# One fused attention and Fourier-mixing kernel: the planner's constants, one new rule for GpSimd, and the instruction order that follows from them

## The chip, the core and the metric

The kernel runs on one core of one Trainium2 chip. The metric is the device time of one execution in microseconds; 672.24 us is the median of three runs of the kernel before (668.16 to 672.58).

## What is computed

The first half is a delta-rule recurrence for 4 batches of 8 heads (768 steps, head size 48), the second half mixes its output by Fourier transforms and sends it through a two-layer MLP. All of it is float32.

```python
for t in range(S):                       # deltanet, per batch and head
    y[t] = q[t] @ state
    v_old = state.T @ k_n[t]             # k_n: k over its norm
    state = state + beta[t] * outer(k_n[t], v[t] - v_old)
# bridge: heads side by side -> x (4, 768, 384)
mixed = real(fft(fft(x, axis=1), axis=2))
u = x + mixed
un = (u - mean(u)) / sqrt(var(u) + 1e-6)
out = u + maximum(un @ w_ch1, 0) @ w_ch2   # 384 -> 1536 -> 384
```

## The kernel before

**Tiles.** The recurrence is done in chunks. A unit is 128 steps of one batch with all 8 heads, two chunks of 64; there are 24 units, six per batch, and six buffers `us` for them. Units go through in rounds: round 0 has units 0 to 3, round 1 units 4 and 5 (together batch 0), rounds 2 to 7 three units each.

**Stages of a round.** K and Q are turned on TensorE (`turn`, transposes, L480), the products of keys and queries are made (`gram`, `keys`, results cleared by L696, L707 and copies at L486), and a triangular system is inverted on VectorE by a long chain of small instructions: `begin16`/`invert16` for rounds 0 and 1 (transposes L795, pairs L855 and L861, transposes L881 and L878), `begin`/`invert` for the others (L751, L766, pairs L933 and L938, L950). `blocks`, `ahead`, `step` and `outputs` then use the inverse unit by unit (L960, L966, L1190, L1219, L1254).

**Batch 0.** It has its own chain, `chain0`: eleven updates of the state, one after another. Each is a small matmul of the state (`st,R`), a copy of two halves of `u` out of PSUM, a matmul of keys and `u`, and a copy of the new state `st` (both copies at L486 on ScalarE, or L488 on VectorE). After the last output (`x`, L486) come the mixing of batch 0 (folds L1279, matmuls with `tab` and `ft`, statistics L1393, scaling L1409, transposes of `pm`) and its MLP, groups of twelve matmuls `R,w` (first layer) and eight `w,R` (second layer) as the hardware counts them: a float32 matmul of the program is two on the chip, a transpose one. The same follows for batches 1 to 3, and matmuls of the MLP are laid between the small matmuls of the next batch's recurrence.

**The weights.** `w_ch1` and `w_ch2` come as 64-bit numbers in 18 pieces of 512 columns. A piece is loaded into a staging place on the SP queue, then converted: L1795 and L1801 on ScalarE, L1798 and L1806 on VectorE, an addition on GpSimd (L1811), and L1814 on VectorE. GpSimd does little else. `where` (L1986) gives the staging place: the first `NW` = 8 pieces use a ring of seven places in `ws`, `x1`, `R1` and `R0`, the others a ring of three. From the eighth piece on a transfer is cut in rows 0 to 120 and 121 to 127 (L1786).

**The order.** No engine's order is written by hand. Every operation is given to `Plan` with a duration for each engine that may run it, its reads and writes, its PSUM banks and a due time; `schedule` walks through planned time and gives each free engine the ready operation with the least `pr`, and `issue` emits all in that order. Each engine then runs its list in order, whatever the real times are. Some rules are built in:

- a VectorE operation marked `port` (a conversion of weights, some folds) is not started while GpSimd's addition runs, and the other way round;
- PE may wait for a better operation that is nearly ready (`PLOOK`, `PHOLD`);
- where PE has nothing ready for `GAP` (inside the listed spans) or `GAP2`, or its activity over the last `SPANW` microseconds falls below `TARGET` (`FORCE` before 20 us), a filler is issued (L2036, L2043): a matmul whose result nobody reads, to keep up TensorE's clock. Before `HALF` the filler may be a pair of 64 rows;
- `speed` doubles planned PE time in windows of 3.413 us after one with too little activity.

Due times come from `due_a` and `due_m` with the constants `M0` to `MD`; `pick` chooses between small and large matmuls with `WAIT`, `GATHER`, `URGENT`.

Of the kernel before, what the change touches and what calls it, by code (L numbers as in the profile page):

```python
# [29 lines left out]
SHARE = 0.3  # L30
RATE = 190.0
WIN, WARM, COLD, BUSY, CLOCK = 3.413, 610.0, 619.0, 200.0, True
LOOK, HOLD, EARLY = 1e9, 0.2, 25.7
FOLD, BY, SEQ, HOT, HOTPE, HOTPK, HOTG, NORM = 1, 1, 2, 1.0, 1, 1, 0, 1
HOTC, PORT, E2 = 2, 1, 5.0
GAP, HALF = 0.198, 68.4
LATE = 0.0
GAP2 = 0.304
PLOOK, PHOLD, PEND = 23.4, 0.367, 116.9
NHALF = 1  # L40
FORCE = 540.9
BLOCK, LEAD, SEEK, LAND, HOLDUP = 256, 60, 1.0, 2.4, 0.0
CUT, ROW = 512, 121
PLAIN, W1T = {(2, 2): (0, 1, 2, 3, 4, 5), (3, 2): (4, 5)}, 0.112
WF = 2, 2
TARGET, SPANW = 692.9, 2.6


class Plan:
# [102 lines left out]
    def light(self, now):  # L152

        a = now - SPANW
        self.past = [p for p in self.past if p[1] > a]
        return sum(c * (min(e, now) - max(s, a)) for s, e, c in self.past) < (TARGET if now > 20 else FORCE) * SPANW

    def schedule(self, pick, limits, switch, idle=None, span=()):
# [15 lines left out]
        free = {e: 0.0 for e in self.ENG}  # L174
# [8 lines left out]
                    avail[e].append(o)  # L183
        self.win, self.sum, self.cold, self.past, self.hist = 0.0, 0.0, True, [], []
        self.count, self.come = 64, [0.0, 0.0]
        self.bursts = []
        done, n, now = 0, len(ops), 0.0
        order, strict, last = [], True, None
        while done < n:
            progressed = False  # L190
            for e in self.ENG:
# [52 lines left out]
                elif cand:  # L244
# [10 lines left out]
                    if best and strict and LOOK and e in ("DVE", "ACT"):  # L255

                        x = now + best.engs[e] - HOLD
                        y, z = best.pr - (LOOK if now > EARLY else 1.0), best.pr - HOT
# [5 lines left out]
                    continue  # L264
                o = best
                dur = o.engs[e]
                if e == "PE":
                    dur *= self.speed(now)
                    if mode is not None:
                        dur += switch.get((mode, o.mode), 0.0)  # L270
                    mode = o.mode
                    for b, s in zip(o.new, fr[len(o.new), o.mode] if o.new else ()):
                        b.slot, slots[s] = s, None
                        self.half = {k: x for k, x in self.half.items() if x != s}
                        held[b.cls] = held.get(b.cls, 0) + 1
# [39 lines left out]
            if not progressed:  # L315
# [7 lines left out]
                now, strict = min(nxt, default=now), bool(nxt)  # L323
# [55 lines left out]
def kernel(  # L379
# [36 lines left out]
    P = Plan(nc, tc, 8)  # L416
# [39 lines left out]
    def A(t, c0, c1, p0=0, p1=128):  # L456
        t, o = parts.get(id(t), (t, 0))
        c0, c1 = c0 + o, c1 + o
        return (id(t), p0, p1, c0, c1)
# [10 lines left out]
    def eng(e):  # L470
        return {"DVE": nc.vector, "POOL": nc.gpsimd, "ACT": nc.scalar, "SP": nc.sync}[e]

    def I(x):
        kp(x)
# [17 lines left out]
    def t_dve(n, ps=False):  # L492
        return 0.07 + n * 1.04e-3

    def t_act(n):
        return 0.07 + n * 0.84e-3

    def t_pool(n):
        return 0.20 + n * 1.9e-3
# [23 lines left out]
    def dma(o, i, wr, pr, rd=(), kb=200, q="SP"):  # L523
        def fn(e):
            I((nc.sync if q == "SP" else nc.scalar).dma_start(out=o, in_=i))
        P.op({q: 0.45}, fn, rd, wr, pr, lat=2.0, kb=kb)


    M0, MP, MX, MN, MA, MT, MD = 91.8, 128.0, 19.9, 38, 17.7, 5.85, 4.52

    def due_a(b, T):
        if b == 0:
# [65 lines left out]
    def pads(ap, acc, pr):  # L598
        def fn(e):
            I(eng(e).memset(ap, 0.0))  # L600
        P.op({"POOL": 0.3, "DVE": 0.2}, fn, [], [acc], pr, lat=LP)
# [1159 lines left out]
    nw = [0]  # L1761

    def weights(src, dst, rows, cols, where, pr, pieces=None):


        n = 512
        if src.dtype == F32:
            d = dst.rearrange("p (c f) -> p c f", c=rows)
            for r in sorted({c0 // cols for c0 in pieces}):
                dma(d[:, r], src[128 * r:128 * r + 128, :], [A(dst, cols * r, cols * r + cols)], pr)  # L1770
            return
        sv = src.bitcast(I32).rearrange("(c p) (f two) -> p (c f) two" if False else
                                        "(c p) f2 -> p c f2", p=128)
        for c0 in pieces:
            w0 = where(nw)
            nw[0] += 1
            st = w0[0][:, w0[1]:w0[1] + 2 * n]
            a0 = A(w0[0], w0[1], w0[1] + 2 * n)
            cc = dst[:, c0:c0 + n]
            ac = A(dst, c0, c0 + n)  # L1780
            rr = st[:, 0:2 * n:2]
            done = 0
            while done < n:
                r, c = divmod(c0 + done, cols)
                m = min(n - done, cols - c, CUT)
                for x0, x1 in ((0, ROW), (ROW, 128)) if nw[0] > 7 else ((0, 128),):  # L1786
                    dma(st[x0:x1, 2 * done:2 * done + 2 * m].bitcast(I32),
                        sv[x0:x1, r, 2 * c:2 * c + 2 * m],
                        [A(w0[0], w0[1] + 2 * done, w0[1] + 2 * done + 2 * m, x0, x1)], pr,
                        kb=m * (x1 - x0) / 128)  # L1790
                done += m
            lo, hi = st[:, 0:2 * n:2], st[:, 1:2 * n:2]

            def f0(e, cc=cc, hi=hi):
                I(nc.scalar.activation(cc, hi, ACT.Abs))  # L1795

            def f1(e, cc=cc):
                I(eng(e).tensor_scalar(cc, cc, LB, UB, op0=ALU.max, op1=ALU.min))  # L1798

            def f2(e, rr=rr, lo=lo):  # L1800
                I(nc.scalar.activation(rr.bitcast(I32), lo.bitcast(U32), ACT.Copy,  # L1801
                                       scale=2.0 ** -29))

            def f3(e, cc=cc):
                w = cc.bitcast(I32)
                I(nc.vector.tensor_scalar(w, w, 5, 2, op0=ALU.logical_shift_left,  # L1806
                                          op1=ALU.logical_shift_right))

            def f4(e, cc=cc, rr=rr):
                w = cc.bitcast(I32)  # L1810
                I(nc.gpsimd.tensor_tensor(w, w, rr.bitcast(I32), op=ALU.add))  # L1811

            def f6(e, cc=cc, hi=hi, c0=c0):
                I(nc.vector.scalar_tensor_tensor(  # L1814
                    dst[:, c0:c0 + n].bitcast(I32), hi.bitcast(I32), -2 ** 30, cc.bitcast(I32),
                    op0=ALU.bitwise_and, op1=ALU.bitwise_xor))
            P.op({"ACT": t_act(n) + 0.07}, f0, [a0], [ac], pr, lat=LA)
            P.op({"DVE": 0.38}, f1, [], [ac], pr, lat=LD, port=True)
            P.op({"ACT": t_act(n) + 0.07}, f2, [], [a0], pr, lat=LA)
            P.op({"DVE": 0.40}, f3, [], [ac], pr, lat=LD, port=True)  # L1820
            P.op({"POOL": t_pool(n) + 0.2}, f4, [a0], [ac], pr, lat=LP, port=True)
            P.op({"DVE": t_dve(n) + 0.03}, f6, [a0], [ac], pr, lat=LD, port=True)
# [3 lines left out]


    nb = [0]
    NW, IV, IV1, WP = 8, 18.9, 9.07, -14.4

    dma(pack, cn["pack"].ap(), [PK], -300, q="ACT", kb=130)
    dma(bt, beta.rearrange("b h s -> (b h) s"), [aBT], -250, q="ACT", kb=98)
# [3 lines left out]
    pads(half, A(half, 0, 1), 0)  # L1836
    for w in p_:
        pads(w, A(w, 0, 256), -400)

    def eps(e):  # L1840
        I(eng(e).memset(half, 1e-6))
# [27 lines left out]
    def mixing(b):  # L1869
        pr = 0  # L1870
        P.hot = True
        for t in range(TH):
            folds(b, t, pr)
        tag = [(("last", b), 0, 1, 0, 1)]
        for i in range(2):
            seq(b, i, pr, tag)
        for T in range(NT):
            feat(b, T, pr)
        for g in range(NT // 2):
            for T in (2 * g, 2 * g + 1):  # L1880
                normed(b, T, pr)
            P.hot = False
            if (b, g) >= WF:
                if b == B - 1:
                    mlpw(b, g, pr)
            else:
                mlp(b, g, pr)
            P.hot = g < HOTG
        P.hot = False
# [35 lines left out]
    def consume(ro):  # L1925
        for i, z in enumerate(ro.us):
            pr = 0
            blocks(z, i, ro, pr)
            ahead(z, pr)
            step(z, 0, pr)  # L1930
            step(z, 1, pr)
            outputs(z, pr)
            if z.T == NT - 1 and z.b:
                if z.b == B - 1:
                    sums1(0)
                    for g in range(NT // 2):
                        if (B - 2, g) >= WF:
                            mlpw(B - 2, g, 0)
                mixing(z.b)
# [46 lines left out]
    def where(nw):  # L1986
        return stages[nw[0] % 7] if nw[0] < NW else stages[(nw[0] - NW) % 3]
# [9 lines left out]
        consume(ro)  # L1997

    LIM = {"state": 1, "sum": 4, "attn": 6, "mix": 4, "mlp": 4, "norm": 2, "win": 4}
    WAIT, GATHER, URGENT, FIRST = 6.3, 1.59, 8.45, 15  # L2000
    E0, E1, D1 = 1.0, 10.0, 125.6
    seen = {}

    def pick(cand, mode, now, free):
# [24 lines left out]
    def idle(two, mode, now):  # L2029
# [3 lines left out]
        def fn(e):  # L2033
# [12 lines left out]

    SW = {("128", "64"): 0.1, ("64", "128"): 0.21, ("128", "T"): 0.1, ("T", "128"): 0.05,
          ("64", "T"): 0.15, ("T", "64"): 0.1}
    P.schedule(pick, LIM, SW, idle, ((E0, D1),))
    P.issue()  # L2050


# [28 lines left out]
```

## Time and profile before

| what | value |
|---|---|
| runs | 672.58, 668.16, 672.24 us |
| the profiled execution's own time | 667.22 us |
| its span, first to last instruction | 665.4 us |
| PE busy, VectorE busy, ScalarE busy, GpSimd busy | 650.6, 504.1, 270.3, 36.3 us |
| granted TensorE clock, mean | 0.997 |
| instructions | 23378 |

A busy PE is not PE at its peak: matmuls are pipelined and their ends are modelled. So times between the starts of matmuls are used as well. Times in the views are counted from the span's start. The engines are PE (matmuls) with PEld (weight loads), DVE (VectorE), ACT (ScalarE), POOL (GpSimd) and SP, whose queue issues the transfers. "x" is a number of instructions.

### The profile page before, as it was taken

To read this page: it belongs to the slowest core of one execution; us is meant where nothing else is said; L and a number is where in the kernel's file an instruction comes from. 1 tells how busy PE (TensorE), PEld (TensorE's weight loads), DVE (VectorE), ACT (ScalarE), POOL (GpSimd) and SP (SyncE) were. 2 spreads that over 40 slices of the span, in tenths; PEclk is the share of its full clock that TensorE was granted. 3 is DMA by queue.
4 is the path that set the end of the run, shared out by engine and by line. 5 is a ranking of instruction groups with operands and counts; after the bars stand their busy time and mean duration, and the time that the engine had idled before them with its cause. 6 is when DMAs were issued, how large, how long until landed. Compare 5 with 4: busy or idle time off the path is not lost.

```text
span 665.4 us, 23378 instructions
## 1 busy us (share of the span) xinstructions
PE 650.6 (98%) x10184; PEld 535.8 (81%) x10184; DVE 504.1 (76%) x1479; ACT 270.3 (41%) x758; POOL 36.3 (5%) x34
## 2 busy tenths in 40 slices
PE   8998899999899999999999999999999999999998
PEld 7888888777678777877777778777777789999997
DVE  3998589999964399999922589998981865877473
ACT  5579787621354332524333433244324313321220
POOL 3004223130000000000000000000000000000000
PEclk9999899999999999999999999999999999999999
DMA  9905565100033113001212120000000000000000
GB/s 201 304 33 105 146 142 148 35 0 25 1 63 75 38 26 73 1 1 26 63 38 50 50 49 2 24 2 3 26 2 3 26 3 0 25 1 25 1 25 25
DMA packets 82667, 31.38 MB, mean 47 GB/s; under 512 B 75651, under 2 KB 79716, under 8 KB 82436
## 3 DMA queue, kind: packets, MB, share of 16 engines
q1 hardware_dynamic: 82372, 29.65, 18.0%
q8 instruction: 80, 1.31, 0.8%
q10 hardware_dynamic: 192, 0.23, 0.1%
q14 instruction: 23, 0.19, 0.1%
HBM read 25.16 MB, written 4.72 MB: 45 GB/s over the span
## 4 chain that ended last, share of the span: by engine, by line
PE 80%; DVE 13%; ACT 3%; issue 2%; DMA 1%; DVEq 0%; SPq 0%; ACTq 0%
PE pp L477 75%; PE pp L480 3%; DVE rr L938 2%; DVE tmp L933 2%; ACT us L486 1%; PE pp L2043 1%; PE pp L2036 1%; DMA x<-in_moe_w_ch_dram 1%; DVE rr L795 1%; DMA us<-in_q_dram 1%; DVE tmp L855 1%; DVE w L861 1%; DVE us L714 0%; ACT w L1795 0%; DVE us L696 0%
## 5 line engine op out<-in xcount | busy, mean ns | idle before, releaser
L477 PE MATMUL pp<-R,w 128*128 128x256 f32 (+1 forms) x832 | 184.1, 368 | 0.6 <-ACT R L486 0.6
L477 PEld LDWEIGHTS pp<-R,w 128*128 128x128 f32 x832 | 145.1, 190 | 19.7 <-ACT R L486 0.7
L477 PE MATMUL pp<-w,R 128*128 128x384 f32 x384 | 135.1, 495 | 0.0
L477 PEld LDWEIGHTS pp<-w,R 128*128 128x128 f32 x384 | 70.0, 190 | 41.0 <-issue 0.2
L486 ACT ACTIVATE us<-pp 128x256 f32<-128x256 f32 (+3 forms) x186 | 65.0, 388 | 61.6 <-PE pp L477 48.3
L1475 ACT ACTIVATE R<-pp 128x512 f32<-128x512 f32 x48 | 28.7, 597 | 106.8 <-PE pp L477 106.8
L477 PE MATMUL pp<-us 64*64 64x48 f32 (+3 forms) x2496 | 61.7, 235 | 1.6 <-issue 1.3
L938 DVE TENSOR_TENSOR rr<-rr,tmp 128x108 f32<-128x108 f32 (+13 forms) x180 | 57.6, 330 | 2.3
L477 PEld LDWEIGHTS pp<-us 64*64 64x64 f32 (+1 forms) x2496 | 52.3, 136 | 8.7 <-issue 5.5
L933 DVE TENSOR_TENSOR tmp<-rr 128x210 f32<-128x210 f32 (+12 forms) x180 | 57.3, 328 | 2.1
L1190 DVE TENSOR_TENSOR u<-u,pp 64x192 f32<-64x192 f32 x66 | 22.4, 351 | 39.3 <-PE pp L477 37.7
L477 PEld LDWEIGHTS pp<-u,us 64*64 64x64 f32 x1472 | 39.7, 134 | 14.7 <-issue 10.5
L477 PE MATMUL pp<-u,us 64*64 64x48 f32 x1472 | 45.7, 221 | 2.8 <-issue 1.3
L486 ACT ACTIVATE x<-pp 64x192 f32<-64x192 f32 (+1 forms) x81 | 25.2, 324 | 54.2 <-PE pp L477 50.1
L1254 DVE TENSOR_TENSOR x<-x,pp 64x192 f32<-64x192 f32 x66 | 23.2, 351 | 24.5 <-PE pp L477 23.3
L486 ACT ACTIVATE R<-pp 128x192 f32<-128x192 f32 (+7 forms) x80 | 22.5, 333 | 43.0 <-PE pp L477 21.8
L1650 DVE TENSOR_TENSOR us<-us,pp 128x256 f32<-128x256 f32 x64 | 26.7, 418 | 12.5 <-ACT us L486 10.3
L477 PE MATMUL pp<-tab,R 128*96 128x193 f32 (+2 forms) x192 | 33.0, 328 | 0.1
L477 PEld LDWEIGHTS pp<-st,us 48*64 48x64 f32 x1232 | 22.6, 134 | 12.3 <-issue 9.8
L477 PEld LDWEIGHTS pp<-tab,R 128*96 128x96 f32 (+2 forms) x192 | 30.8, 163 | 1.4 <-DVE R L1279 0.6
L2043 PE MATMUL pp<-pack 64*64 64x256 f32 (+1 forms) x206 | 31.1, 384 | 0.0
L486 ACT ACTIVATE u<-pp 64x192 f32<-64x192 f32 (+1 forms) x68 | 22.2, 326 | 17.0 <-PE pp L477 11.7
(165 smaller groups left out, 978.1 us busy)
## 6 DMA issues: line engine op xcount, KB each, us to landing
out_dram<-x SPq DMA_DIRECT2D x11, 384.0 KB
us<-in_k_dram SPq DMA_DIRECT2D x16, 192.0 KB
us<-in_q_dram SPq DMA_DIRECT2D x16, 192.0 KB
us<-in_v_dram SPq DMA_DIRECT2D x16, 192.0 KB
us<-in_v_dram SPq DMA_DIRECT2D x8, 181.5 KB
ws<-in_moe_w_ch_dram SPq DMA_DIRECT2D x3, 484.0 KB
us<-in_k_dram SPq DMA_DIRECT2D x8, 181.5 KB
us<-in_q_dram SPq DMA_DIRECT2D x8, 181.5 KB
```

What stands on the lines that cost most here:

```text
L477: I(nc.tensor.matmul(o, lhsT=lhsT, rhs=rhs, start=start, stop=stop, skip_group_check=True))
L480: I(nc.tensor.matmul(o, lhsT=src, rhs=ident[p0:p0 + n, p0:p0 + n], is_transpose=True, start=start, stop=True, skip_group_check=True))
L486: I(nc.scalar.activation(o, i, ACT.Copy, **({} if scale is None else {"scale": scale})))
L795: vec(1760, lambda e: I(nc.vector.transpose(R, ro.gd(0, 4).rearrange("p (n c) -> p c n", c=32))), [ro.agd(0, 4)], [aR], pr)
L855: I(eng(e).tensor_tensor(T_, sub(j + 1, 16, j, j + 1).broadcast_to([128, 2, n, j]), sub(j, j + 1, 0, j).broadcast_to([128, 2, n, j]), op=A ...
L933: I(eng(e).tensor_tensor(T_, R[:, :, j + 1:32, j:j + 1].broadcast_to([128, ns, n, j]), R[:, :, j:j + 1, 0:j].broadcast_to([128, ns, n, j]) ...
L938: I(eng(e).tensor_tensor(R[:, :, j + 1:32, 0:j], R[:, :, j + 1:32, 0:j], T_, op=ALU.add))
L1190: I(nc.vector.tensor_tensor(U[:, s], U[:, s], psum(b1[s])[a, s0:s1].rearrange("p (j d) -> p j d", d=D), op=ALU.subtract))
L1254: I(nc.vector.tensor_tensor(w, w, v, op=ALU.add))
L1475: I(nc.scalar.activation(o, s, ACT.Relu))
L1650: vec(256, lambda e: I(nc.vector.tensor_tensor(o, i0(), i1(), op=ALU.add)), [], [aH] + list(wr), pr - EV, use=n)
L2043: I(nc.tensor.matmul(pst[two[0]][x, 0:256], lhsT=w[x, 0:n], rhs=w[x, 0:256], start=True, stop=True, skip_group_check=True))
```

## The change

About twenty constants of the planner get other values. A new rule adds 0.9 us (`CHARGE`) to the planned duration of the first VectorE operation without a PSUM bank that starts while GpSimd's addition runs. A second span, 250 to 280 us of planned time, is treated as the first one is: there PE's activity is watched and fillers are issued after shorter gaps. In `consume`, `blocks` and `ahead` of the second and third unit of a round are made more urgent by 4.3 us each. The ring of seven staging places now serves the first 15 pieces of the weights; the row cut begins after the seventh piece or the `NW`-th, whichever is less.

```diff
-LOOK, HOLD, EARLY = 1e9, 0.2, 25.7
+LOOK, HOLD, EARLY = 1e9, 0.204, 22.8
...
-GAP, HALF = 0.198, 68.4
+GAP, HALF = 0.198, 71.5
...
-PLOOK, PHOLD, PEND = 23.4, 0.367, 116.9
+PLOOK, PHOLD, PEND = 58.7, 0.317, 115.6
...
-FORCE = 540.9
+FORCE = 579.1
 BLOCK, LEAD, SEEK, LAND, HOLDUP = 256, 60, 1.0, 2.4, 0.0
+CHARGE = 0.9
...
-TARGET, SPANW = 692.9, 2.6
+TARGET, SPANW = 690.0, 2.6
...
-        self.bursts = []
+        self.bursts, self.lock = [], 1e9
...
+                if e == "POOL" and o.port:
+                    self.lock = now + 0.2
+                if e == "DVE" and not o.banks and self.lock < now < free["POOL"]:
+                    self.lock, dur = 1e9, dur + CHARGE
...
-    M0, MP, MX, MN, MA, MT, MD = 91.8, 128.0, 19.9, 38, 17.7, 5.85, 4.52
+    M0, MP, MX, MN, MA, MT, MD = 86.9, 139.9, 29, 37.9, 19.8, 5.91, 5.44
...
-                for x0, x1 in ((0, ROW), (ROW, 128)) if nw[0] > 7 else ((0, 128),):
+                for x0, x1 in ((0, ROW), (ROW, 128)) if nw[0] > min(7, NW) else ((0, 128),):
...
-    NW, IV, IV1, WP = 8, 18.9, 9.07, -14.4
+    NW, IV, IV1, WP = 15, 18.9, 6.6, -14.4
...
+    BL = 4.3
...
-            blocks(z, i, ro, pr)
-            ahead(z, pr)
+            blocks(z, i, ro, -BL * i)
+            ahead(z, -BL * i)
...
-    WAIT, GATHER, URGENT, FIRST = 6.3, 1.59, 8.45, 15
-    E0, E1, D1 = 1.0, 10.0, 125.6
+    WAIT, GATHER, URGENT, FIRST = 5.29, 2.53, 5.88, 15
+    F0, F1 = 250.0, 280.0
+    E0, E1, D1 = 1.0, 10.0, 129.8
...
-    P.schedule(pick, LIM, SW, idle, ((E0, D1),))
+    P.schedule(pick, LIM, SW, idle, ((E0, D1), (F0, F1)))
```

In what follows line numbers are those of the kernel before; in the kernel after the same lines stand 5 to 7 lines further down.

## The prediction

> **What bounds the kernel now.** First the page's table of slices, to see where an engine is full:
>
> ```profile
> PE   8998899999899999999999999999999999999998
> DVE  3998589999964399999922589998981865877473
> ACT  5579787621354332524333433244324313321220
> PEclk9999899999999999999999999999999999999999
> ```
>
> From the eleventh slice on (about 170 us) PE is full and DVE and ACT are not always: there the kernel is bound by PE's work. Ahead of that DVE and ACT are as full as PE. The busy times of five stretches, cut at steps that I use below, and of two pairs of short windows:
>
> ```profile
> 0.00:49.90 49.90, 46.21 (x1112) 40.18 (x1112) 38.84 (x147) 31.55 (x86) 7.25 (x11) 1.00 0.68 179
> 49.90:99.40 49.50, 45.33 (x1536) 41.58 (x1540) 37.44 (x78) 41.60 (x116) 14.83 (x13) 0.97 0.57 131
> 99.40:120.60 21.20, 20.36 (x298) 17.76 (x293) 20.18 (x53) 17.01 (x53) 5.47 (x4) 1.00 0.46 120
> 120.60:176.40 55.80, 54.02 (x286) 38.69 (x282) 55.38 (x168) 14.35 (x39) 7.86 (x4) 1.00 0.05 17
> 176.40:665.40 489.00, 484.72 (x6970) 397.55 (x6970) 352.28 (x1038) 165.76 (x468) 0.94 (x3) 1.00 0.11 25
> ...
> 74.60:78.00 3.40, 2.10 (x86) 1.97 (x77) 1.70 (x4) 2.30 (x8) 0.85 (x1) 1.00 0.74 163
> 78.20:81.60 3.40, 3.40 (x99) 3.28 (x98) 1.10 (x3) 2.44 (x8) 0.23 (x1) 0.50 0.72 215
> ```
> ```profile
> 275.96:279.38 3.42, 2.41 (x21) 1.86 (x21) 3.38 (x13) 1.44 (x5) 0.00 (x0) 1.00 0.00 0
> ```
>
> The columns after the length are PE, PEld, DVE, ACT, POOL, then granted clock. A busy PE is not a PE at its peak, so I made a ledger: each matmul of the program gets the mean time from its start to the next start, by form, over the part after 100 us; fillers get nothing. That is 610.2 us of work in a span of 665.4: 55.2 us are lost (fillers, idle PE, sparse issue). Lost by 49.9 us (chain0's first matmul) 28.9; by 99.4 (its last, state with unit 5) 44.3; by 120.6 (first MLP matmul) 48.1; by 176.4 (round 2's first use of its inverse) 48.6. The last 489 us lose only 6.6. So what can be won lies ahead of 120 us, above all between 50 and 99, where 15.4 us are lost.
>
> What ends the waits there, from the timelines of ACT, PE, POOL and DVE:
>
> ```profile
> 77.25 0.68 PE L477 MATMUL pp<-u,us 64*64 64x48 f32 x19 [1.30 <-issue]
> ```
> ```profile
> 104.89 0.68 ACT L1795 ACTIVATE w<-x 128x512 f32<-128x512 f32 x1 [2.38 <-DMA x<-in_moe_w_ch_dram]
> ```
> ```profile
> 176.38 1.20 PE L477 MATMUL pp<-t,us 64*32 64x32 f32 x64 [1.78 <-DVE t L966]
> ```
> ```profile
> 46.63 1.47 POOL L1811 TENSOR_TENSOR w<-w,ws 128x512 int32<-128x512 int32 x1 [40.33 <-ACT us L486]
> ```
> ```profile
> 31.69 0.18 DVE L855 TENSOR_TENSOR tmp<-w 128x28 f32<-128x28 f32 x1
> ...
> 46.87 1.27 DVE L855 TENSOR_TENSOR tmp<-w 128x28 f32<-128x28 f32 x1
> ```
>
> The reader is to see: a PE that lacks instructions (issue), ACT held by a weight transfer, one wait of PE for DVE, and an instruction of DVE that takes 1.27 us instead of 0.18 because GpSimd's addition started 0.24 us earlier. Over the 18 additions such holds come to about 11 us of DVE, most of them 1.0 to 1.1 us; a third of the additions have none.
>
> **The change part by part.** Both kernels' compiled order shows the same 5230 matmuls; fillers go from 105 to 112. I price each engine's list ahead of a step by the medians of this trace.
>
> *Transfers.* The row cut begins after piece 7 in both (min(7, 15) is 7): SP has 155 transfers in both, of the same sizes. This line does nothing. The ring for 15 pieces does: eight pieces are staged in R0 and R1 rather than in ws and x1, and are issued on SP ahead of round 2's K and Q: four transfers of 0.33 us issue each before the first, six more before the second unit. SP stands there until L1814 of the piece in R1 is done (59.2 in this trace, 9.0 us of DVE work earlier in the new list). Round 2's K is issued at 55 and first used at 78 us; 3.3 us later it is still in time. Cost 0; if that cover goes, PE's turns wait, at most those 3.3 us.
>
> *Up to chain0.* DVE has 0.9 us more ahead of the inverse of round 0 (27.5 to 28.4 us of listed work: three scalings L714 of 0.54 and others moved forward). DVE is busy 20.1 of 21 us from 14 to 35, so this lies on the path: +0.9. PE's 1.1 us more of work there falls where fillers stood (72 fillers ahead of the first `gd,w` in both): nothing.
>
> *Chain0.* At its last state matmul (99.4) PE's list holds 2.9 us less work than before (52.2 for 55.1), DVE's list 2.9 less ahead of the last fold, ACT's 0.2 less ahead of the last output. Less work done by then is work owed later: the ledger gets +2.9, less x, by which the chain ends earlier. What x is the trace of before can't show. It is at most 2.9 (both lists shorter) plus 1.7 (the window at half clock: 3.41 us at 0.50) plus 1.5 (two of the holds and of the issue waits of 0.5 to 1.3): 6.1. It is at least -6.0: in the middle, at the sixth state copy (72.8), ACT's list is 6.0 longer, ACT is nearly full from 35 to 71 (32.7 of 36), and it has 6.9 idle in 71 to 102 to give that back. I take 2.9, the difference of the two lists that are shorter, since the idle of ACT covers its excess at the end (0.2 less).
>
> *99 to 121 us.* ACT's conversion of the piece that it waited for moves forward by nine places; the idle 0.84 and the filler pair 0.97 at 100 to 103 have other work: PE has 1.6 less behind it at 120.6 for 2.9 at 99.4, so 1.3 of the debt is paid: -1.3.
>
> *To 176 us.* PE's work ahead of round 2's first use is exactly the same, 127.8. DVE's list ahead of that inverse is 8.4 us shorter (round 3's start is moved behind it), so the wait of 1.78 goes: -1.8. What is late next, round 3's inverse, has the same list on DVE and 7.8 us more PE work ahead of its use: no wait.
>
> *The tail.* Same work; changes between large, small and transposing matmuls go from 172 to 175 at about 0.1 us: +0.3. Around batch 1's mixing there are seven fillers for three; a filler costs 0.54 (the pairs took 0.63, 0.54, 0.46). Seven are 3.8; three and the idle 0.42 and 0.59 there were 2.6: +1.2, between -1.0 (all in idle time) and +2.2.
>
> Sum: 0.9 + 2.9 - x - 1.3 - 1.8 + 0.3 + 1.2 = 2.2 - x. With x = 2.9 that is -0.7: 667.2 - 0.7 = 666.5 for the profiled execution's own 667.22 (span 665.4 and 1.8 around it). That execution was the fastest shown; the median of the runs, 672.24, lies 5.0 above. What those runs lose no trace shows, so I take nothing for it and forecast 666.5, which is 0.9% under the median: no change by the bound of 1%, about what a measurement of this kernel can tell.
>
> **The clock.** The windows show that after one busy 2.10 of 3.40 us the clock was 0.50 for 3.41, and after one busy 2.41 (275.96) it was 1.00. So that place stands 0.3 us from a loss of 1.7. There the new order puts one filler between the transposes and the first MLP matmul, into the idle 0.59. In this execution it wins nothing; where the window falls worse, 1.7. The Trainium skill ("TensorE: Matmul & The Clock Gate", What's actually happening) lets the clock fall only after a whole idle window of about 3.4 us. The trace disagrees: the longest idle stretch ahead of the slow window was 1.3 us. By that rule the four fillers protect nothing in any execution and the sum stays as it stands.
>
> **Rivals.**
> - *Chain0 comes in early* (x = 6.1, no slow window, fewer holds): 667.2 + 2.2 - 6.1 = 663.3. For it: DVE has a hole from 70 to 90 (10.2 busy of 20) which the new staging fills with conversions, and ACT's waits of 2.38 and 0.65 for transfers go. Against it: the issue waits and the holds are not tied to the order; L855 follows an addition twice in the new list where it did once.
> - *ACT makes chain0 late* and ends slower: its place is 50 to 75 us, where state copies stand behind up to 6.0 us more of conversions and of `u` and `x` copies in ACT's list. If nothing is given back x is -6.0: 667.2 + 8.2 = 675.4, 1.2% over the profiled execution. Against the median it decides at 679, x under -9.6, or with the 5.0 of the slower runs on top.
> - *It does little*: where PE is bound the work is the same to 0.3 us, and x = 2.2 leaves 667.2.
>
> **Chances.** The forecast, with the third rival beside it (664 to 671), 0.52; early chain0 0.28; late chain0 0.20. Faster by over 1% (under 665.5): 0.28 and 0.07 of the forecast's lower end, 0.35. Slower by over 1% (over 679): half of late chain0, 0.10. Within 1%: 0.55. The range reaches to the early rival with the tail's -1.0 in place of +1.2 and two more holds saved (about 659.5) and to the late one (676).
>
> **What would show it.** In the profile after: chain0's last `st,us` near 97 us (before 99.4) confirms x = 2.9; near 94 the early rival, past 102 the late one. No wait of PE for L966 near 175. From round 2's first use to the end 489 us, within 2. Fillers at 250 to 280: seven. Long L855 or L933 beside additions stay about as many. The prediction is wrong if the last stretch changes by more than 2 us, or if ACT's list holds the state copies.

## The result, and the profile after

| | before | after |
|---|---|---|
| runs of the first comparison | 22 | 22 |
| median, us | 670.86 | 674.12 |
| lowest, highest | 665.55, 680.57 | 669.47, 680.68 |
| ratio, 95% interval | | 1.0057, 1.003 to 1.0085 |
| profiled execution: time, span | 667.22, 665.4 | 672.73, 670.9 |
| its mean granted clock | 0.997 | 0.990 |

The kernel after is 0.57% slower: within the 1% that was called no change, but on the other side of the forecast (666.5 on the scale of the profiled execution, where it is 672.73, and 0.7 us faster in place of 5.5 slower). A second set of 12 runs gave 1.0026 (0.9991 to 1.0061).

The page's slices of after, then the five stretches, cut at the same matmuls as those of before (columns as there):

```profile
PE   8999899999999999999999999999999999999998
DVE  4998658999994269999942459989992765967573
ACT  6589667713255234421634233335324213222120
PEclk9999779999999999999999999999999999999999
```
```profile
0.00:50.90 50.90, 47.35 (x1153) 41.00 (x1156) 39.69 (x150) 33.48 (x90) 8.05 (x12) 1.00 0.68 176
50.90:102.40 51.50, 46.93 (x1460) 42.45 (x1454) 35.24 (x63) 38.65 (x111) 16.11 (x13) 0.87 0.57 133
102.40:123.40 21.00, 20.62 (x302) 18.24 (x297) 19.33 (x59) 15.53 (x50) 4.79 (x3) 1.00 0.41 103
123.40:179.20 55.80, 55.80 (x333) 40.06 (x331) 54.38 (x158) 16.42 (x45) 4.39 (x4) 1.00 0.05 18
179.20:670.90 491.70, 485.99 (x6979) 399.09 (x6978) 352.99 (x1044) 167.85 (x476) 0.93 (x3) 1.00 0.11 25
```

The clock row has two 7s where before had one 8: the second stretch, chain0, ran at 0.87. It holds 1460 matmuls for 1536 and is 2.0 us longer. The last stretch is 2.7 us longer (491.7 for 489.0). Chain0 in steps of one clock window, and what PE waited for there:

```profile
66.81:70.22 3.41, 2.05 (x64) 1.90 (x62) 3.38 (x8) 2.41 (x8) 1.41 (x2) 1.00 0.79 192
70.22:73.64 3.42, 3.42 (x90) 3.08 (x84) 2.34 (x5) 2.31 (x7) 2.12 (x3) 0.50 0.64 108
73.64:77.05 3.41, 3.41 (x158) 3.24 (x157) 2.54 (x7) 2.65 (x9) 1.83 (x2) 1.00 0.50 143
77.05:80.46 3.41, 1.61 (x46) 1.24 (x41) 1.40 (x1) 1.40 (x5) 2.54 (x2) 1.00 0.32 63
80.46:83.87 3.41, 3.41 (x54) 2.37 (x54) 2.23 (x5) 2.31 (x6) 0.65 (x1) 0.50 0.72 176
83.87:87.28 3.41, 3.41 (x92) 3.41 (x88) 1.52 (x1) 1.73 (x6) 0.97 (x1) 0.50 0.16 44
87.28:90.70 3.42, 3.42 (x109) 3.26 (x104) 0.00 (x0) 1.09 (x5) 0.00 (x0) 0.50 0.50 100
```
```profile
69.41 0.67 PE L482 MATMUL pp<-st,R 48*64 48x48 f32 x16 [1.36 <-ACT st L491]
...
79.15 0.31 PE L482 MATMUL pp<-u,us 64*64 64x48 f32 x2 [1.80 <-issue]
```

Four windows at half clock (one in before's profile), first one and then three in a row, each time behind a thin one, in which PE has little to do (2.05 and 1.61 busy): ahead of the first PE waits 1.36 for the state, ahead of the three stands a stop of issue of 1.80 in the middle of a state update. That made the clock the first suspect.

### The profile page after: what moved, and what is told of

Its sections match the earlier page's. It is cut to its first block, busy times and chain, and to the rows that moved or that the text cites. A ratio compares the mean times of both kernels' runs of the same rounds, so it can differ in the third digit from the quotient of the medians.

```text
span 670.9 us, 23404 instructions
## 1 busy us (share of the span) xinstructions
PE 656.7 (98%) x10198; PEld 540.8 (81%) x10198; DVE 501.6 (75%) x1469; ACT 271.9 (41%) x768; POOL 34.3 (5%) x34
## 4 chain that ended last, share of the span: by engine, by line
PE 94%; DVE 3%; ACT 2%; issue 1%; ACTq 0%
PE pp L482 87%; PE pp L485 3%; PE pp L2050 3%; PE pp L2043 1%; DVE w L1803 0%; DVE w L866 0%; DVE tmp L860 0%; ACT us L491 0%; DVE rr L800 0%; ACT gd L491 0%; DVE w L826 0%; DVE us L719 0%; DVE w L833 0%; ACT w L491 0%; ACT R L491 0%
## 5 line engine op out<-in xcount | busy, mean ns | idle before, releaser
L491 ACT ACTIVATE us<-pp 128x128 f32<-128x128 f32 (+3 forms) x188 | 65.7, 392 | 72.6 <-PE pp L482 52.8
L482 PE MATMUL pp<-us 64*64 64x64 f32 (+3 forms) x2496 | 62.8, 236 | 3.9 <-issue 2.7
L482 PEld LDWEIGHTS pp<-us 64*64 64x64 f32 (+1 forms) x2496 | 53.7, 137 | 11.0 <-issue 6.6
L938 DVE TENSOR_TENSOR tmp<-rr 128x234 f32<-128x234 f32 (+13 forms) x180 | 57.6, 328 | 2.3
L943 DVE TENSOR_TENSOR rr<-rr,tmp 128x234 f32<-128x234 f32 (+13 forms) x180 | 56.9, 325 | 2.5
L482 PEld LDWEIGHTS pp<-u,us 64*64 64x64 f32 x1472 | 41.7, 139 | 17.0 <-issue 15.3
L482 PE MATMUL pp<-u,us 64*64 64x48 f32 x1472 | 47.5, 226 | 2.3 <-issue 2.3
L491 ACT ACTIVATE R<-pp 128x192 f32<-128x192 f32 (+5 forms) x82 | 23.4, 337 | 36.9 <-PE pp L482 20.4
L2050 PE MATMUL pp<-pack 64*64 64x256 f32 (+1 forms) x220 | 36.6, 391 | 0.7 <-ACT R L491 0.4
L1224 DVE TENSOR_TENSOR st<-st,pp 128x192 f32<-128x192 f32 x30 | 10.6, 354 | 27.7 <-PE pp L482 27.2
```

The lines of the kernel that those rows point to most:

```text
L482: I(nc.tensor.matmul(o, lhsT=lhsT, rhs=rhs, start=start, stop=stop, skip_group_check=True))
L491: I(nc.scalar.activation(o, i, ACT.Copy, **({} if scale is None else {"scale": scale})))
L938: I(eng(e).tensor_tensor(T_, R[:, :, j + 1:32, j:j + 1].broadcast_to([128, ns, n, j]), R[:, :, j:j + 1, 0:j].broadcast_to([128, ns, n, j]) ...
L943: I(eng(e).tensor_tensor(R[:, :, j + 1:32, 0:j], R[:, :, j + 1:32, 0:j], T_, op=ALU.add))
L1224: I(nc.vector.tensor_tensor(sn[:, s0:s1], so[:, s0:s1], psum(b2)[:, s0:s1], op=ALU.add))
L2050: I(nc.tensor.matmul(pst[two[0]][x, 0:256], lhsT=w[x, 0:n], rhs=w[x, 0:256], start=True, stop=True, skip_group_check=True))
```

## The experiments

Every run reports its span and mean granted clock. One window of 3.41 us at 0.50 lowers the mean by 0.0025, so the clock counts the windows of runs that have no trace. A straight line through a kernel's runs gives its span at one common clock, 0.9925 (errors are standard errors; runs over 700 us, and one below 0.95, are left out):

| kernel | runs | mean clock | mean span | span at 0.9925 |
|---|---|---|---|---|
| before | 117 | 0.9896 | 670.1 ±0.3 | 668.5 ±0.1 |
| after (two sets) | 34 | 0.9896 | 672.4 ±0.5 | 670.5 ±0.3 |
| a_fill | 12 | 0.9928 | 671.4 ±0.9 | 671.5 ±0.5 |
| b_fill | 12 | 0.9929 | 669.3 ±1.1 | 669.5 ±0.6 |
| a_nopool | 11 | 0.9929 | 669.4 ±0.9 | 669.6 ±0.4 |
| b_nopool | 11 | 0.9875 | 669.5 ±1.2 | 666.6 ±0.7 |
| a_notail | 11 | 0.9885 | 671.4 ±0.9 | 668.9 ±0.5 |
| a_last | 12 | 0.9852 | 674.3 ±0.9 | 670.7 ±0.7 |
| b_idle (two sets) | 24 | 0.9922 | 668.8 ±0.8 | 668.7 ±0.3 |

Names with a_ start from after, with b_ from before. An order was edited once the planner had made it (`P.order`), so the rest stays as it was.

**b_again**: before, unchanged.

> The kernel before, unchanged, to learn how its runs spread over the granted clock. The 22 runs of the kernel after have spans from 667.7 to 678.9 us and mean clocks from 0.997 to 0.982; a straight line through them falls by 1.65 us for each 0.0025 of clock, which is one window of 3.41 us at half clock in 671. Theory CLOCK (the new order loses because more such windows fall into chain0): the runs of before lie on the same line within 1 us (about 667 to 668 at 0.997) and have a higher mean clock than after, 0.9925 or more for after's 0.989. Theory LISTS (the new order is slower at any clock, by late work on ScalarE and VectorE and by added fillers): the mean clock is the same, 0.989, and before's line lies 3 us lower.

Ratio 1.0033 (0.9994 to 1.0073): a kernel against itself may differ by 0.3%. With all runs of before the two kernels have the same mean clock, 0.9896, and before's line lies 2.0 ±0.3 lower. The clock theory, in the form that after simply has more slow windows in a run, is refuted; where in the kernel they fall is another matter.

**a_fill, b_fill**: five filler pairs more, at thin places of chain0 (`extra` puts pairs ahead of the operation of that number on PE).

```diff
     P.schedule(pick, LIM, SW, idle, ((E0, D1), (F0, F1)))
+    extra({314: 2, 344: 3})     # a_fill
+    extra({331: 2, 346: 3})     # b_fill
     P.issue()
```

> The kernel after with its order kept and five filler pairs more: two ahead of the state matmul that waits 1.36 us for ScalarE at 69.4, three ahead of the 16 matmuls of u and us that stop for 1.80 us of issue at 77.1. Both stand in the windows ahead of those at half clock. A pair took 0.46 to 0.63, so the five cost 2.7 us if nothing covers them. CLOCK: one to three windows go, the mean clock rises from 0.989 to about 0.993, and the ratio to the kernel before falls from 1.0057 to about 1.001 to 1.003. LISTS: nothing is won, the ratio is 1.006 to 1.010.

> The kernel before with its order kept and five filler pairs more at its two thin places: two ahead of the matmuls of us and pb that stop for 0.92 us at 64.4, three ahead of the matmuls of u and us that stop for 1.30 us at 75.7, ahead of its one window at half clock. CLOCK: the mean clock rises to about 0.997 and the ratio is 0.995 to 0.999. LISTS: the clock has little to give, the pairs cost their 1 to 2.7 us, ratio 1.001 to 1.004.

a_fill 1.0029 (0.9985 to 1.0072), b_fill 1.001 (0.9966 to 1.0053). Both clocks rise by 0.0033, 1.3 windows, and at a common clock both take 1.0 us more (±0.6). What they save (1.8 to 2.1 us at 1.4 to 1.6 a window) and what they cost nearly cancel; neither ratio can be told from no change. By its ratio a_fill came out as CLOCK had it, b_fill as LISTS had it, so the pair does not decide. In a_fill's profile one window is left in chain0, yet the chain still ends 1.4 us later than in after (103.3 for 101.9): a stop of issue of 2.12 us stands ahead of 72.99.

**a_nopool, b_nopool**: GpSimd's additions left out.

```diff
+    P.order = [o for o in P.order if not (o.eng == "POOL" and o.port)]
```

> The kernel after without GpSimd's 18 additions in the conversion of the weights (that part of the conversion is left out), all else in the same order. It takes away every hold of VectorE, 16.6 us of longer VectorE instructions in the trace of after and 11 in before, among them the pair of conversions of 2.96 us at 64.4 that makes gd, then ScalarE's copies and the state 1.36 us late. LISTS: 3 us or more are won at the same mean clock (0.989). CLOCK: what is won comes with a higher clock, since the wait ahead of the first window goes; the fetch stall at 77.1 stays, so the clock rises to about 0.992 and 1.5 to 2 us are won; ratio 1.002 to 1.004.

> The kernel before without GpSimd's 18 additions (that part of the weights' conversion is left out). The same cut gave the kernel after 1.2 +-0.5 us at the same clock and 1.3 +-0.6 fewer windows at half clock. HOLDS (they are what the new order pays): before gains 0.5 us or less at the same clock and no windows. Rival: it gains as much as after did, and the holds do not tell the two orders apart.

a_nopool 0.9996 (0.9954 to 1.0038), b_nopool 1.0000 (0.9953 to 1.0048). At a common clock the holds cost after 0.9 ±0.5 and before 1.9 ±0.7 us: the order made with `CHARGE` does not pay more for them there. After gained clock as well, before did not, and in the plain means the two kernels without additions take the same (669.4 ±0.9 and 669.5 ±1.2). So the holds do not explain the difference at a common clock, but that they have a part in the 2.3 us of the means, by way of the clock, is not excluded. b_nopool's profile is a warning besides: PE's order is before's, yet it stopped for 2.43 us of issue ahead of 83.25, four slow windows followed (84.6 to 98.2), and the last state matmul began at 105.0 (98.9 in before).

**h_ba, h_ab, h_aba**: the two orders joined at places where they have nearly the same operations behind them (44 and 105 us planned), written out as a list in place of the planner's.

```diff
-    P.schedule(pick, LIM, SW, idle, ((E0, D1), (F0, F1)))
+    P.order = ...
```

> Every engine's order as in the kernel before for the planned first 105 us (up to the end of chain0), from there on as in the kernel after; transfers of the weights staged as before. So far, at the same mean clock of 0.9925 (straight lines through the runs), the kernel before has a span of 668.4 +-0.2 and the kernel after 670.5 +-0.3. Theory CHAIN0 (the new order loses in chain0, between 44 and 105 us, and wins a little behind it): at that clock 666.6 to 668.4, as the wait of 1.8 for L966 goes and the fillers at 250 to 280 cost up to 1.2 and a stop of issue at 215 0.9. Theory TAIL (the order behind chain0 loses what the fillers, mode changes and stops of issue cost): 670 to 671.

> The other half: orders and staging as in the kernel after up to the end of chain0 (106 us planned), then as before. CHAIN0: 670.5 to 671.5 at a clock of 0.9925, no better than after, since chain0 is late (first 53, last state matmul about 102 for 99) and the wait for L966 comes back. TAIL: 668 to 669, as before.

> The kernel after with only the stretch of chain0 (44 to 105 us planned) ordered as before. CHAIN0: the loss lies in this stretch, so 667 to 668.5 at a clock of 0.9925, 2 to 3 us under after; its last state matmul near 99. If instead the first 44 us carry it (more work of PE ahead of chain0: 24.4 for 22.2 us), 670 or more and chain0 begins at 53 and ends at 101 or later. TAIL: 670.5 as after.

Ratios 1.0108 (1.0054 to 1.0162), 1.014 (1.0075 to 1.0205) and 1.005 (1.0013 to 1.0086): both theories missed. In h_ba and h_ab the seams cost more than the halves differ; for h_aba no profile shows where its time goes. PE's longest waits from 105 to 135 us, h_ba first, h_ab second:

```profile
PE pp L477 <- ACT R L486: 4.4, 1, 4.4
```
```profile
PE pp L485 <- ACT ss L491: 6.0, 1, 6.0
```

The mixing of batch 0 is late where one engine's list was planned against another past; then four and two windows at half clock follow (117.7, 123.9). So this way does not split the 2 us. The profile of h_ab is of use all the same: up to 106 us planned its order is after's. It had one window in chain0 (69.3), as many as before's profile, and its last `st,R` began at 97.2, 1.7 us ahead of before's.

**a_notail, a_last**: after without the fillers at 250 to 280, and with only the last of them.

```diff
+    P.order = [o for o in P.order if not (o.i == -1 and 200 < o.start < 300)]   # a_notail
+    P.order = [o for o in P.order if not (o.i == -1 and 200 < o.start < 273)]   # a_last
```

> The kernel after without the fillers that the second span adds at 250 to 280 us (7 go), the order else the same. Prediction's term: they cost 1.2 us (bounds -1.0 to 2.2), so 669.3 at a clock of 0.9925 in place of 670.5. TAIL: the larger end, 2 us or more. CHAIN0: no more than 1.2. What they were for: where they are missing a window at half clock may fall at 278 to 284, as it does in three of the profiles of the kernel before and its variants so far (two of three), so the mean clock may fall by up to 0.0025.

> The kernel after with one of the seven fillers around batch 1's mixing kept, the last, which stands in the idle ahead of the first MLP matmul. Without all seven the span at a clock of 0.9925 was 668.9 +-0.5, with them 670.5 +-0.3, and a window fell at 283.7. If the last one alone is enough for the clock: 669 at that clock, mean clock 0.0895 plus 0.9 (0.9895 or more, as after), ratio to before about 1.002 to 1.003. If not: mean clock 0.9885 as without them.

1.0026 (0.9988 to 1.0063) and 1.0055 (1.0018 to 1.0092). At a common clock the one is 1.6 ±0.6 below after, the other 0.2 ±0.8 above, though they differ by one filler; the price of the seven stays between nothing and 2. What they protect shows in the profiles. a_notail has a window at 283.7, a_last at 288.0; after, a_again and a_fill, with all seven, have none behind 100 us. From a_notail's windows:

```profile
280.30:283.71 3.41, 1.55 (x15) 1.23 (x16) 3.41 (x13) 1.41 (x6) 0.00 (x0) 1.00 0.01 2
283.71:287.12 3.41, 3.41 (x10) 2.70 (x9) 3.41 (x11) 0.32 (x1) 0.00 (x0) 0.50 0.00 0
```

**a_again**: after, unchanged.

> The kernel after, unchanged, for a second profile and its runs' clocks beside those of before on the same chip. Theory NET (the two orders differ by about 2 us at the same clock, and the new one has its windows at half clock in chain0 where the old one has them at 175 to 180 and near 280): mean clock as before's within 0.001, span 2 us above before's at the same clock, chain0's last state matmul at 100 to 103 us with one to four windows in chain0 and none near 178. Theory CLOCK: mean clock lower than before's by 0.0025 or more, and at the same clock no difference.

As NET has it: mean clock 0.9897, chain0's last state matmul at 101.1, three windows in chain0 (70.77 to 81.01) and no later one. This time the stop of issue fell into the chain's own state matmuls:

```profile
72.20 0.76 PE L482 MATMUL pp<-st,R 48*64 48x48 f32 x9 [1.64 <-issue]
```

**b_idle**: before with three fillers where PE stands idle anyway; run twice.

```diff
+    extra({908: 2, 1338: 1})     # whole fillers of 128 rows
```

> The kernel before, order kept, with three fillers in places where PE stands idle anyway: two in the 1.78 us ahead of the first use of round 2's inverse (174 us), one in the 0.59 us ahead of batch 1's first MLP matmul (277.5 us). Two of three profiles of before's order had a window at half clock right behind the second place, one of three behind the first. They cost nothing at the same clock if the idle covers them (at most 0.5 us). NET: about one window of 1.4 to 1.7 us is saved in a run, mean clock up by 0.002, ratio 0.996 to 0.999. Rival: the windows come from the phase of the clock's grid and move elsewhere; ratio 1.000 or more.

> The kernel before with the three fillers in its two idle places, a second time: the first gave a ratio of 0.9947 (0.9909 to 0.9986), 2.4 windows a run for 4.2 and no cost at the same clock. If that holds: ratio 0.993 to 0.998, mean clock 0.992 or more. If it was the phase of that call: 0.999 or more and mean clock 0.9895.

0.9947 (0.9909 to 0.9986), then 1.0011 (0.9966 to 1.0056). At a common clock it costs nothing (668.7 for 668.5). The windows are 3.1 ±0.5 a run for before's 4.2 ±0.2, so the first gain was mostly that set of runs'; that this version beats both kernels is possible but not shown. Both its profiles are free of slow windows until the last 3 us. Before's second profile (b_again) shows what the places can do:

```profile
175.00:178.41 3.41, 1.63 (x66) 1.36 (x66) 3.41 (x11) 0.63 (x2) 0.31 (x1) 1.00 0.00 0
178.41:181.83 3.42, 3.42 (x9) 2.68 (x9) 3.18 (x10) 0.86 (x3) 0.00 (x0) 0.50 0.02 5
277.40:280.81 3.41, 2.40 (x22) 1.90 (x22) 3.37 (x13) 1.48 (x6) 0.00 (x0) 1.00 0.00 0
280.81:284.22 3.41, 3.41 (x9) 2.72 (x9) 3.41 (x11) 0.00 (x0) 0.00 (x0) 0.50 0.00 0
```

**b_late**: does work taken out of PE's list end the chain earlier? Four groups of matmuls of round 2, with their copies and clears, are moved behind chain0's last state matmul; the order is written out as for h_ba.

> Tests the step that the prediction took (what leaves PE's list ahead of chain0's end lets the chain end as much earlier): the kernel before with the turns and products of round 2's first unit (four groups of matmuls, planned at 3.1 us, and their copies and clears) moved from within chain0 to behind its last state matmul. If work in the list is what times the chain, its last state matmul moves from 98.9 (99.8 in the second profile) to about 96. If the chain is timed by its own latency, stops of issue and the clock, it moves by less than 1 us. Round 2 then starts later: the wait for L966 at 174 grows, so the whole is slower, by up to the delay of about 15 us less what VectorE has spare; ratio 1.00 to 1.02.

Ratio 1.0108 (1.0056 to 1.016), as expected from the late round 2. The last state matmul began at 97.8, inside the 97.2 to 99.8 of the four profiles of before's chain0: 3.2 us less priced work between its first and last state matmul (29.6 for 32.8), and the chain took 47.1 us for 46.6 to 47.8. Like before's profile (47.8) it had one slow window in chain0, so 3.2 us less work shortened the chain by 0.7. The list alone does not time the chain; the last state matmul stood in a wait for the state's copy.

```profile
97.83 0.67 PE L477 MATMUL pp<-st,R 48*64 48x48 f32 x16 [1.45 <-ACT st L486]
```

**a_convlate, b_convlate**: are it the conversions? All that are planned in chain0 are moved behind it.

> The kernel after with all conversions of weights that are planned between 58 and 95 us (and the transfers behind them) moved behind chain0's last state matmul, so that ScalarE, VectorE and GpSimd have nothing but chain0 and round 2's start there. Only chain0 is read from it; the first MLP then waits for its weights, so the whole is slower by 10 us or more. Theory HOLDS (conversions and GpSimd's holds on VectorE make chain0 late): its last state matmul (101.9, 101.1, 102.1 and 105.1 in the profiles of the kernel after and its variants with the same chain0) moves to 97 or earlier. Theory PE (PE's own list, stops of issue and the clock time it): it stays at 100 or later.

> The same with the kernel before (conversions planned between 56 and 95 us moved). HOLDS: the chain's end moves less than in the new order, from 98.9 by 1 to 2 us, as the old order has fewer holds there. PE: it stays within 1 us of 97.2 to 99.8.

Slower by 1.0409 (1.033 to 1.0488) and 1.0403 (1.0324 to 1.0483), since the MLP then waits for its weights. The chains end where they did: last state matmul at 102.1 and 98.7. HOLDS fails again, at equal numbers of slow windows: with no conversion near, after's chain0 took about 48 us with three slow windows, as in a_again, and before's about 47 with none, as in b_idle. The three, from 68.0, came with a stop of issue:

```profile
68.67 0.53 PE L482 MATMUL pp<-lo,us 64*64 64x32 f32 x5 [2.08 <-issue]
```

## Why the prediction was wrong

**The step that failed is x.** "I take 2.9, the difference of the two lists that are shorter." Chain0 was to end at 97. It ended (last `st,us`) at 102.4 and 101.6 in the two profiles of after, for 99.4 and 100.3 in the two of before: x is -2.2, an error of 5.1 us, more than the errors of all other terms together. In before, after, a_again and h_ab, in this order:

```profile
99.42 0.64 PE L477 MATMUL pp<-st,us 48*64 48x48 f32 x30
```
```profile
102.41 0.65 PE L482 MATMUL pp<-st,us 48*64 48x48 f32 x30
```
```profile
101.62 0.65 PE L482 MATMUL pp<-st,us 48*64 48x48 f32 x30
```
```profile
97.73 0.65 PE L482 MATMUL pp<-st,us 48*64 48x48 f32 x30
```

Of the 2.2 us, 1.6 are a later start (first `st,R` at 52.9 and 53.3 for 51.1 and 51.9) and 0.6 a longer chain. The rival late chain0 had the sign right, and its mark in one profile of two (past 102), but not the cause: ScalarE's list holds a state copy for long only once in after (at 69.04, by about 1 us), and a_convlate took ScalarE's conversions away without effect on the chain's end.

What did it, by my count of the stretch from the first to the last `st,R` (each interval between matmul starts is put down to priced work, idle PE, fillers, half clock, or what is left, which is sparse issue):

| us | before | b_idle | after | a_again |
|---|---|---|---|---|
| length | 47.8 | 46.6 | 48.9 | 47.8 |
| priced work | 32.8 | 32.8 | 27.7 | 27.7 |
| idle | 4.2 | 4.3 | 4.6 | 4.6 |
| fillers | 2.7 | 2.9 | 4.3 | 3.9 |
| half clock | 1.4 | 0.0 | 5.2 | 3.5 |
| sparse issue | 6.7 | 6.7 | 7.2 | 8.0 |

Work fell by 5.1 and the chain is no shorter. Half clock took the largest part of it, then fillers and sparse issue. x took the clock in chain0 as unchanged, and by these profiles most of it failed there: h_ab, after's chain0 with one slow window, took about 45 us and ended 1.7 us ahead of before's, over half of the 2.9; after's chain0 took about 48 with two or three windows (a_notail, a_again), 49 with four (after) and 51 with four and a part of a fifth (a_last). Windows at half clock between 50 and 111 us: 4, 3, 2, 6 and 1 in the five profiles whose chain0 is after's unchanged (after, a_again, a_notail, a_last, h_ab); 1, 0, 0, 0 and 1 in the five whose chain0 is before's (before, b_again, both b_idle, h_ba). The order alone does not fix the number: b_nopool had 4 with before's order on PE, and its chain took about 54. Nor is this an experiment on the clock alone: in a_fill one window was left and the chain took about 49, as five pairs and a longer stop of issue came in. My reading is that a chain whose steps pass from engine to engine leaves PE as thin as its list is short, and that thin PE costs clock: less work in the list is itself a risk, which I had priced at nothing. b_late shows the other half, that a shorter list need not shorten the chain by as much (0.7 for 3.2).

**Why the mean clock is nevertheless the same.** The new order removed two thin places behind chain0 (the wait for L966 and batch 1's mixing; windows in b_again, b_fill and without the fillers) and made chain0 thinner. The profiles show the places; that this exchange also balances over all runs is inferred from the equal means, since the runs without a trace do not tell where their windows lay.

**The other terms, by the ledger** (lost time at the same matmuls, in the order before, b_again, after, a_again):

| at | lost | change forecast | measured |
|---|---|---|---|
| chain0's first | 28.8, 29.1, 28.8, 28.8 | +0.9 | -0.2 |
| its last `st,us` | 44.3, 45.1, 50.2, 49.4 | 2.9 - x = 0 | +5.2 |
| first MLP matmul | 48.1, 48.7, 52.4, 51.9 | -1.3 | -1.4 |
| round 2's `t,us` | 48.5, 49.2, 51.3, 50.8 | -1.8 | -1.5 |
| 300 us | 51.0, 54.5, 56.4, 55.6 | +1.2 | +1.1 |
| last matmul | 51.8, 55.0, 57.0, 56.0 | +0.3 | -0.2 |

Each measured change is the mean of after's two less the mean of before's two, less the row above. As they stand all but x are right within 1.1 us. The first row has b_again's early window (at 14.6) in it; without it, it is +0.7. The 300 us row has b_again's two later windows; without them it is +2.8, of which a stop of issue that no list showed is 0.9 (0.7 in a_again). So the agreement of these two rows is in part luck. The wait for L966 is gone and round 2 starts without idle time (compare 176.38 in before):

```profile
179.17 1.20 PE L482 MATMUL pp<-t,us 64*32 64x32 f32 x64
...
216.03 0.47 PE L482 MATMUL pp<-us 64*64 64x64 f32 x17 [0.93 <-issue]
```

The transfers cost nothing, as said: no wait of PE in after's first 300 us is put down to a DMA. The sign "as many holds" was wrong in size: my count of longer VectorE instructions beside additions is 16.6 us for 11, among them a pair of 0.4 us each:

```profile
64.42 2.96 DVE L1803 TENSOR_SCALAR w<-w 128x512 f32<-128x512 f32 x2
```

Most lie where VectorE has room. This pair does not: `gd` comes behind it at 67.30, ScalarE waits 1.36 for `gd` and goes on at 67.81, and PE's wait of 1.36 for the state, ahead of the first slow window, follows. In a_nopool and a_convlate that wait is gone, yet their last state matmuls begin at 102.0 and 102.1. The last stretch changed by 2.7 us where I had allowed 2. Of the other rivals, early chain0 found no support (no profile of after's chain0 is free of slow windows, and none ends near 94), and "it does little" was right about the part that PE bounds.

**The base.** The forecast stood on one execution of before, its clock 0.997, and was set beside a median: of the 5.7 us between 666.5 and 672.24 only 0.7 were forecast of the change. Its runs have 0.9896 on average, about 3 windows more. What "those runs lose" and "no trace shows" was in the clock of every run, and 5.5 us of profiled difference is 2.3 ±0.6 in the means. What stays open: how the 2.0 us at the same clock divide among fillers (0 to 2), the stop at 216 (0.9 and 0.7 in the two profiles) and sparse issue in chain0, and whether the additions have a part in the rest.

## What to carry to other kernels

Where a chain hops between engines, the difference of two lists does not price the chain: price each of its steps, and ask what a thinner PE does to its clock. Before two profiles are compared, count the slow-clock windows in both and put many runs of each kernel on a line of span against clock; here that turned 5.5 us into 2. Put fillers where PE is idle anyway (b_idle: no cost at the same clock), rather than into a chain (about 1.0 us for five pairs), and do not graft parts of two planned orders together (h_ba and h_ab: 8 us and more above before in the means).

## What the runs showed of the hardware

**The clock falls after windows that are mostly busy, and the busy share alone does not decide.** With PE busy 2.40 of 3.41 us the next window was at 0.50 (b_again, 277.40). At the same place in before it was busy 2.40 as well and the clock stayed; the prediction's 275.96 lies 0.2 us off that execution's clock windows, and the margin of 0.3 us that it read there is none. In the same way 1.63 stayed at 1.00 in before (173.76) and fell in b_again (175.00):

```profile
173.76:177.17 3.41, 1.63 (x52) 0.98 (x52) 3.41 (x8) 0.04 (x1) 0.31 (x1) 1.00 0.00 0
276.16:279.57 3.41, 2.40 (x20) 1.82 (x20) 3.41 (x12) 1.44 (x5) 0.00 (x0) 1.00 0.00 0
```

In a_again 2.44 stayed and 2.46 fell:

```profile
63.94:67.36 3.42, 2.44 (x93) 2.33 (x85) 3.21 (x5) 3.19 (x8) 2.59 (x2) 1.00 0.23 46
67.36:70.77 3.41, 2.46 (x74) 2.21 (x70) 3.38 (x8) 2.24 (x7) 1.42 (x2) 1.00 0.79 176
70.77:74.18 3.41, 1.98 (x37) 1.98 (x38) 2.22 (x4) 0.80 (x3) 2.11 (x3) 0.50 0.48 90
```

Here the window that fell held fewer matmuls (74 for 93), but the number does not decide either: at 1.63 the one with 66 fell and the one with 52 did not. What does is open. And a full window does not always bring the clock back: in after PE was busy through three windows from 80.46 at half clock; the first two, with 54 and 92 matmuls, were followed by another slow one, only the third, with 109, by full clock. The Trainium skill ("TensorE: Matmul & The Clock Gate", What's actually happening) has the clock fall after a whole idle window and return after one busy one. These rows disagree on both. It also calls the window free-running, not tied to the kernel's start; there the traces agree: one and the same order had its slow windows at 78.19 or at 14.57, 178.41 and 280.81.

**Small matmuls outrun instruction fetch.** PE's stops of issue end a short and steady time behind a transfer of instructions. The trace's transfers show one of 16 KB from 76.49 to 77.63 in after; PE stopped at 77.35 for 1.80 and went on at 79.15, 1.5 us behind the landing. In before one came from 74.93 to 75.86; PE stopped at 75.95 for 1.30 and went on at 77.25, 1.4 us behind it. Of the 84 stops of issue over 0.35 us between 45 and 300 us in 17 profiles (all but h_aba's) every one ends 1.2 to 1.8 us behind the landing of such a transfer. The row of that queue on after's page:

```profile
q8 instruction: 80, 1.31, 0.8%
```

Eighty packets of 16 KB; in chain0 there is one about every 4 us, and stops of 0.4 to 2.4 us behind several of them in every profile. The Trainium skill ("Runtime: NRT & Kernel Launch", Instruction fetch mechanics) calls the cost of crossing such a block mostly hidden; for matmuls that start 0.023 us apart, each with its weight load (the mean of the last 100 ahead of the stop at 77.35), it was not.
